# Block-sparse attention with a channel mix: dense units for the two blocks that see every key, two batches in one unit

## Chip, cores and metric

The kernel runs on one core of a Trainium2 chip. The metric is the device time of one execution in microseconds (us); the time before is the median of three runs.

## What is computed

```python
B, H, S, D = 4, 8, 768, 64          # block = 32, so 24 blocks
scores = (1 / sqrt(D)) * (q @ k.transpose(0, 1, 3, 2))
mask = |blk_i - blk_j| <= 1  or  blk_i in (0, 23)  or  blk_j in (0, 23)
for qb in range(24):                 # sampled_blocks: [24, 3], known only at run time
    mask[block qb, block kb] = True  for kb in sampled_blocks[qb]
attn = softmax(where(mask, scores, -1e9))
x = (attn @ v)  as  [B, S, H * D]    # 512 columns
xp = x shifted by one row, zero first
xk = mu_k * x + (1 - mu_k) * xp
xr = mu_r * x + (1 - mu_r) * xp
out = sigmoid(xr @ w_r) * (relu(xk @ w_k) ** 2 @ w_v)
```

Query blocks 0 and 23 see all 24 key blocks. Every other block sees at most eight: its own and its two neighbours, blocks 0 and 23, and three sampled ones. The weights w_r, w_k and w_v arrive as float64 (2, 4 and 4 MB), and the kernel turns them into pairs of fp32r tiles.

## The kernel before

**Units.** Attention is cut into 24 units. A dense unit (`m == ALL`, `load_wide` and `wide_pair`) takes four query blocks of one batch, 128 rows, against all 768 keys; the blocks are `WIDE_BLOCKS`, which are 21, 22, 23 and 0, so there are four dense units, one for each batch b. A gathered unit (`load_near` and `near_unit`) takes two neighbouring query blocks of a pair of batches, also 128 rows, against the eight key blocks that each may see; ten units for each of the two pairs cover blocks 1 to 20.

**A dense unit** goes over four pairs of heads, hp. For each: scores `sw` (PE, one matmul per head and half of the keys), a masked minimum in `soft` (DVE) and the exponential (ACT), twelve transposes `tw` (PE) that are copied to `ptw`, then products with the values, `o_-1_...` (PE). At the end `finish` divides by the row sums and transposes four times, `tx`. **A gathered unit** has 32 score matmuls `s` (64 rows by 32 columns of the array each), `soft`, `exp`, sixteen transposes `t`, 64 value matmuls `o` and four `tx`. Its keys are laid in the tile `KR`, of which there is one: the next unit's keys can only be asked for when `s` of this unit is done. Its values take four of the six tiles `VR`.

**Transfers.** SP issues nearly all of them, in one order. A gathered unit is q (262 KB), the near keys `kd` (524 KB), six sampled key blocks `kt` (131 KB each, at addresses that SP reads from the tile `packed`), two near value tiles `vn` (524 KB) and six sampled value blocks `vt`; when a tile is first used for a pair, blocks 0 and 23 come as well. A dense unit is 3.4 MB: q, four key tiles `k_ring<-kq` of 393 KB, and six value transfers of 262 KB. SP stays at most 2.2 MB ahead of what has landed (`QUEUED`).

**Channel mix.** Each of 12 tiles (128 rows of a pair of batches) has PE work in three parts: gates `r` (w_r), hidden rows `h` (w_k), output rows `v` (w_v). A tile can start when the units of all its blocks are done and the weights it reads are converted; tile 0 of a pair needs block 0 and the units m = 0 and 1.

**Order.** `Plan` sorts all operations by ranks from hand-tuned tables (`UNIT_AT`, `TILE_AT`, offsets `O_...` and `W_...`) and by its own costs and buffer queues; each engine then runs its list in that fixed order. The units come in the order of `UNITS`:

```python
UNITS = [
    (0, ALL), (1, ALL), (2, ALL), (0, 0), (0, 1), (3, ALL), (0, 2), (0, 3), ...
]
```

Dense units of the second pair are thus done early, and their rows for that pair's tiles are parked in HBM (`away`) and read back later.

Of the kernel before, what the change touches and what calls it, by code (L numbers as in the profile page):

```python
# [26 lines left out]
TT = 128  # L27
# [14 lines left out]
WIDE_SCALE = 2.0**-8  # L42

# [54 lines left out]
class Plan:  # L98
# [168 lines left out]
def block_sparse_attention_channel_mix(  # L267
    ctx: ExitStack, tc: tile.TileContext,
    kt, kd, kq, qw, qn, vt, vn, blocks, own_wide, own_near, mu_k, mu_r, w_k, w_v, w_r, out, wide,
# [34 lines left out]
    away = [Fixed(dr.tile([P, CC, P], F32, name=f"away{b}")) for b in range(PAIR, B)]


    def mask_setup():
# [35 lines left out]
        def twice():
# [3 lines left out]
            g = f.ap[:, 1:, :]  # L347
# [15 lines left out]
        plan.add(DVE, 1150, -30, far, reads=[(own,)], writes=[(f, 0), (same,), (wide_mask,)])  # L363
        plan.add(DVE, 2900, TWICE, twice, reads=[(con,)], writes=[(f, 1), (same,), (near_mask,)])
# [744 lines left out]
```

## Time and profile before

| | |
|---|---|
| three runs | 576.47, 576.67, 579.05 us (median 576.67) |
| profiled execution | span 575.5 us, from its first to its last instruction; its own time is not given apart, and the fastest and the median run lie 1.0 and 1.2 us above this span |
| PE (TensorE matmul) | 557.4 us busy, 97% of the span |
| DVE, ACT, POOL | 293.3, 298.2, 297.6 us busy, 51 to 52% |
| transfers | 102.91 MB, mean 179 GB/s |

PE is the matmul pipe, PEld its weight loads, which overlap with it. SPq rows are transfers that SP issues. A PE instruction counts as busy from its start to its modelled end, so neighbours overlap by 0.07 us or so; from the start of one group to the start of the next is what the group takes.

### The profile page before, as it was taken

Reading aid. Unit: us, or ns where it says so; the run is one execution under the profiler, and the core shown is the slowest. Engines: PE = TensorE matmul, PEld = TensorE weight load, DVE = VectorE, ACT = ScalarE, POOL = GpSimd, SP = SyncE. Lnnn points to the kernel's source line nnn. Section 1 sums busy time; section 2 is a strip of 40 time slices with the busy share of each in tenths; the row PEclk is TensorE's granted clock in tenths of the full one; section 3 lists DMA queues with packets and bytes.
Section 4 is the critical chain, followed back from the end, with each engine's and each line's share of the span. In section 5 each row is a group of like instructions: output and inputs, shape, how many; then the busy total and the mean of one; then the engine's idle time right before and its main releaser. Section 6 shows DMA issues by size and latency. Waiting matters only on the chain.

```text
span 575.5 us, 18316 instructions
## 1 busy us (share of the span) xinstructions
PE 557.4 (97%) x7203; PEld 461.1 (80%) x7203; DVE 293.3 (51%) x855; ACT 298.2 (52%) x719; POOL 297.6 (52%) x367
## 2 busy tenths in 40 slices
PE   8999877999999999999999999999999999999997
PEld 4777655788889888889889879888989888888886
DVE  4978786878872643445556454546314323230201
ACT  4688755758853736536736634544523344414420
POOL 0143546766655715607607605635428778867720
PEclk9999998999999999999999999999999999999999
DMA  8997789688898747766776577476302100010001
GB/s 297 403 305 270 233 279 344 210 269 298 266 288 251 208 144 211 229 206 200 236 220 194 174 238 228 143 234 182 97 20 84 39 0 1 17 45 12 2 18 56
DMA packets 52152, 102.91 MB, mean 179 GB/s; under 512 B 9345, under 2 KB 26626, under 8 KB 52066
## 3 DMA queue, kind: packets, MB, share of 16 engines
q1 hardware_dynamic: 51778, 101.51, 54.8%
q8 instruction: 57, 0.93, 0.6%
q14 instruction: 29, 0.24, 0.1%
q10 hardware_dynamic: 288, 0.22, 0.1%
HBM read 94.89 MB, written 6.82 MB: 177 GB/s over the span
## 4 chain that ended last, share of the span: by engine, by line
PE 80%; DVE 2%; POOL 1%; ACT 0%; issue 0%
PE v L895 24%; PE t L581 6%; PE o L643 6%; PE s L612 5%; PE r_0p L835 5%; PE r_1p L835 4%; PE h_1p L861 4%; PE h_2p L861 4%; PE h_0p L861 4%; PE h_3p L861 4%; PE tx L705 1%; PE o_-1_1567 L686 1%; PE h_1p L877 1%; PE h_5p L877 1%; PE h_4p L877 1%; PE r_3p L835 1%
## 5 line engine op out<-in xcount | busy, mean ns | idle before, releaser
L895 PE MATMUL v<-wv,k 128*128 128x512 f32 (+1 forms) x600 | 139.8, 389 | 0.3 <-ACT z L842 0.3
L895 PEld LDWEIGHTS v<-wv,k 128*128 128x128 f32 x600 | 108.2, 188 | 27.0 <-issue 1.6
L570 ACT ACTIVATE p<-p,nm 128x256 f32<-128x256 f32 x160 | 79.4, 498 | 15.1 <-DVE nm L560 15.0
L587 DVE COPY pt<-t 128x512 f32<-128x512 f32 x80 | 53.2, 684 | 59.7 <-PE t L581 48.3
L560 DVE CUSTOM_DVE_ANT_1 p<-s,near_mask 128x256 f32<-128x256 f32 x160 | 57.8, 419 | 14.0 <-PE s L612 10.7
L903 DVE SCALAR_TENSOR_TENSOR z<-v,z 128x512 f32<-128x512 f32 (+1 forms) x25 | 16.7, 670 | 71.8 <-PE v L895 52.6
L811 POOL TENSOR_TENSOR xr<-xr_1f,xr 128x256 fp32r<-128x256 f32 x24 | 18.2, 758 | 67.6 <-ACT xr L809 67.5
L581 PE MATMUL t<-ident,p 128*128 128x128 f32 x320 | 48.5, 285 | 4.0 <-DVE pt L587 2.4
L581 PEld LDWEIGHTS t<-ident,p 128*128 128x128 f32 x320 | 44.4, 206 | 6.8 <-ACT xt L720 1.7
L612 PE MATMUL s<-KR,q 64*32 64x256 f32 x1280 | 40.3, 379 | 2.1 <-DMA KR<-kt 1.9
L643 PEld LDWEIGHTS o<-VR,pt 128*32 128x32 f32 x2560 | 37.0, 110 | 5.3 <-issue 2.9
L643 PE MATMUL o<-VR,pt 128*32 128x64 f32 x2560 | 40.9, 220 | 0.2 <-DMA VR<-vt 0.2
L802 DVE SCALAR_TENSOR_TENSOR xr_1f<-xr_1d,mk,xt 128x128 f32<-128x128 f32 x48 | 19.5, 445 | 40.6 <-POOL xr L811 36.0
L802 DVE SCALAR_TENSOR_TENSOR xr_0f<-xr_0d,mk,xt 128x128 f32<-128x128 f32 x48 | 20.0, 452 | 33.0 <-POOL xr L811 28.3
L570 ACT ACTIVATE pw<-pw,nmw 128x768 f32<-128x768 f32 x32 | 30.0, 938 | 12.2 <-DVE nmw L560 12.1
L612 PEld LDWEIGHTS s<-KR,q 64*32 64x32 f32 x1280 | 24.6, 106 | 10.7 <-DMA KR<-kt 2.5
L835 PE MATMUL r_0p<-wr,xr 128*128 128x512 f32 x120 | 31.0, 403 | 0.0
L835 PE MATMUL r_1p<-wr,xr 128*128 128x512 f32 x120 | 30.5, 401 | 0.0
L570 ACT ACTIVATION_READ_ACCUMULATOR p<-p,nm 128x1 f32 x160 | 30.0, 188 | 0.0
L664 PE MATMUL sw<-k_ring,qw 64*128 64x384 f32 x128 | 27.5, 539 | 2.5 <-DVE x L708 1.1
L581 PE MATMUL tw<-ident,pw 128*128 128x128 f32 x192 | 27.7, 281 | 2.2 <-ACT ptw L585 1.6
L581 PEld LDWEIGHTS tw<-ident,pw 128*128 128x128 f32 x192 | 20.6, 141 | 10.6 <-ACT ptw L585 3.7
(188 smaller groups left out, 1079.5 us busy)
## 6 DMA issues: line engine op xcount, KB each, us to landing
VR<-vn SPq DMA_DIRECT2D x40, 512.0 KB, 4.6
VR<-vt SPq DMA_DIRECT2D x127, 128.0 KB, 4.0
KR<-kt SPq DMA_DIRECT2D x120, 128.0 KB, 3.3
KR<-kd SPq DMA_DIRECT2D x20, 512.0 KB, 4.2
VR<-vt SPq DMA_DIRECT2D x24, 256.0 KB, 7.0
out<-z SPq DMA_DIRECT2D x23, 256.0 KB, 2.3
k_ring<-kq SPq DMA_DIRECT2D x15, 384.0 KB, 6.1
q<-qn SPq DMA_DIRECT2D x20, 256.0 KB, 3.6
```

The lines of the kernel that those rows point to most:

```text
L560: nc.vector.tensor_tensor_reduce(out=p.ap[:, cs].rearrange("p (x n) -> p x n" if inner else "p (n x) -> p n x", **cut), in0=view().rearran ...
L570: plan.add(ACT, 378 + 0.83 * (cs.stop - cs.start), rank, lambda: nc.scalar.activation(p.ap[:, cs], p.ap[:, cs], AF.Exp, bias=nm.ap[:, col ...
L581: nc.tensor.transpose(tp.ap[:, i, :], cs(p.ap), ident.ap)
L587: plan.add(DVE, 690, rank + 0.1, lambda: nc.vector.tensor_copy(out=pt.ap, in_=tp.ap), reads=[(tp,)], writes=[(pt,)])
L612: nc.tensor.matmul(s.ap[ROWS[j], row, a * 256 : (a + 1) * 256].rearrange("p (x a g) -> p g a x", g=2, a=QB), q.ap[half, hp, ROWS[j]], eigh ...
L643: nc.tensor.matmul(o.ap[ROWS[j], h * D : (h + 1) * D], held[gi][i // 2].ap[:, 2 * (i % 2) + g, ROWS[j]], VR[values[j % PAIR][g]].ap[:, j / ...
L664: nc.tensor.matmul(s.ap[:, row, 0:W], q.ap[half, hp, :], K.ap[half, n0 * BLK : n0 * BLK + W], start=True, stop=True)
L802: nc.vector.scalar_tensor_tensor(out=part(f.ap[:, i, :]), in0=part(d.ap), scalar=mk.ap[:, which, c : c + 1], in1=x.ap[:, two, c, 0:TT], op ...
L811: plan.add(POOL, 80 + 2.4 * MIX * tw, rank + O_MIX, lambda f=f, cs=cs: nc.gpsimd.tensor_tensor(out=dst.ap[:, 1, cs], in0=f.ap, in1=dst.ap[ ...
L835: nc.tensor.matmul(pr.ap[:, 0:512], xr.ap[:, a, c, :], wr.ap[:, w, c, :], start=(c == 0 and m == 0), stop=(c == CC - 1 and m == 2))
L861: nc.tensor.matmul(ph.ap[:, ff * PAIR * TT : (ff + 1) * PAIR * TT], wk.ap[:, w, c, f * P : (f + 1) * P], xk.ap[:, a, c, :], start=(c == 0 ...
L895: nc.tensor.matmul(pv.ap[:, 0:width], hid[f][2](a), wv.ap[:, w, f, cs], start=(f == 0 and m == 0), stop=(f == FC - 1 and m == 2))
```

## The change

1. `WIDE_BLOCKS` is (23, 0). Blocks 21 and 22 become an eleventh gathered unit of each pair. A dense unit now takes blocks 23 and 0 of both batches of a pair: 128 rows again, but with the keys and the values of two batches, 6.6 MB. There are two dense units instead of four and 22 gathered ones instead of 20.
2. In a dense unit's scores each matmul covers 64 rows and 64 columns of the array (one batch), so there are four per half of the keys and not two; its value matmuls keep their number and shape and read each half of the columns from another batch's tile.
3. `UNITS` is in plain order: dense unit, then the eleven gathered ones, for each pair. The second dense unit's keys go into `KR` and its values into `VR`, which the gathered units use too. Nothing is parked in HBM any more.
4. `soft` of a gathered unit writes its probabilities so that a transpose reads 128 neighbouring columns (before: every second one).
5. `early` (the space of w_v before w_v is converted) holds keys and values of the second gathered unit; the first twelve raw weights use the `xt` tiles instead. All ranks are new numbers, and the planner's costs for transfers are.

```diff
-WIDE_BLOCKS = (NB - 3, NB - 2, NB - 1, 0)
+WIDE_BLOCKS = (NB - 1, 0)
-NP, NM = B // PAIR, (NB - QB) // PAIR
+NP, NM = B // PAIR, (NB - 2) // PAIR
...
-    FIRST, WORDS, AHEAD, ASKED, FETCHED = 143, 256, 298, 800, 2500
+    FIRST, WORDS, AHEAD, ASKED, FETCHED = 143, 256, 298, 800, 1600
-    RING, RATE, DONE, LANES = 650, 290, 800, 8
+    RING, RATE, DONE, LANES = 1600, 390, 1000, 8
...
-UNITS = [
-    (0, ALL), (1, ALL), (2, ALL), (0, 0), (0, 1), (3, ALL), (0, 2), (0, 3), (0, 4), (0, 5), (0, 6), (0, 7),
-    (0, 8), (0, 9), (1, 0), (1, 1), (1, 2), (1, 3), (1, 4), (1, 5), (1, 6), (1, 7), (1, 8), (1, 9),
-]
+UNITS = [(p, m) for p in range(NP) for m in [ALL, *range(NM)]]
...
+    v_ring = buf([P, V_RING, S], F32, "mixed", 1, "v_ring")
...
-            raw = Part(early, EARLY_W, ...) if i < 3 * CC else buf([P, 512, 2], I32, "p", P_BUFS, f"raw{i}")
+            raw = buf([P, 512, 2], I32, *(("xt", XT_BUFS) if i < 3 * CC else ("p", P_BUFS)), f"raw{i}")
...
+    def wide_key(lead, n):
+        if lead:
+            return Place(Part(k_ring, K_RING, lambda x, i: x[:, i]), [(0,), (1,)], lambda x: x)
+        k = n % K_LATER
+        slots[0][0] = None
+        return Place(KR[0], [(RINGS[k],)] * 2, lambda x: x.rearrange("p n b x -> p (n b x)")[:, k * S : (k + 1) * S])
+    def wide_value(lead, n):
+        if lead:
+            return Place(Part(v_ring, V_RING, lambda x, i: x[:, i]), (0, 1), lambda x: x)
+        w = n % VR_BUFS
+        slots[1][w] = None
+        return Place(VR[w], (0, 1), lambda x: x.rearrange("p b x -> p (b x)")[:, 0:S])
...
             if inner:
+                by = mask().unsqueeze(1).to_broadcast([P, BLK, SLOTS]).rearrange("p x (a g) -> p x a g", g=2)
+                cut = lambda x: x.rearrange("p (x a g) -> p x a g", g=2, a=QB)
+                dealt = lambda x: x.rearrange("p (g x a) -> p x a g", g=2, a=QB)
...
-                parts = [(p, [(i, i * 256)], lambda x, i=i, g=g: x[:, i * 256 : (i + 1) * 256].rearrange("p (y g) -> p g y", g=2)[:, g]) for i in (2 * a, 2 * a + 1) for g in range(2)]
+                parts = [(p, [(i, i * 256)], lambda x, i=i, g=g: x[:, i * 256 + g * P : i * 256 + (g + 1) * P]) for i in (2 * a, 2 * a + 1) for g in range(2)]
...
-                for row, half in enumerate(HALF):
-                    nc.tensor.matmul(s.ap[:, row, 0:W], q.ap[half, hp, :], K.ap[half, n0 * BLK : n0 * BLK + W],
-                                     start=True, stop=True)
+                for one, K in zip(HALF, both):
+                    for row, half in enumerate(HALF):
+                        nc.tensor.matmul(s.ap[one, row, 0:W], q.ap[half, hp, one], K.ap[half, n0 * BLK : n0 * BLK + W],
+                                         start=True, stop=True, skip_group_check=True)
...
-EARLY_W, EARLY_K, K_RING = 4, 0, 5
+EARLY_K, K_RING, V_RING, K_LATER = 2, 5, 5, 4
...
 UNIT_AT = [
-    -75.8943, -50.8142, -29.7091, -3.8416, 4.4692, 49.253, 88.5915, 99.3214, 124.6571,
+    -5.4147, 11.3186, 19.3007, 40.5254, 71.6051, 80.3593, 93.0373, 105.2062, 131.9685,
```

**Where instructions stand.** On PE, at the end of the first dense unit, before: the unit's last values (`o_-1_180`) and its `tx` stand among the scores and transposes of the second dense unit (its query tile is `qw_155`).

```order
L686 MATMUL o_-1_180<-VR_71,ptw_3_2_402 64x64 x4
L686 MATMUL o_-1_180<-VR_72,ptw_3_2_402 64x64 x4
L581 MATMUL tw_0_1_466<-ident,pw_0_0_339 128x128 x2
L581 MATMUL tw_0_1_466<-ident,pw_0_1_349 128x128 x2
L581 MATMUL tw_0_2_475<-ident,pw_0_1_349 128x128 x4
L664 MATMUL sw_2_0_487<-k_ring,qw_155 128x384 x2
L705 MATMUL tx_-1_494<-ident,x_-1_490 128x128 x4
L581 MATMUL tw_1_0_517<-ident,pw_1_0_472 128x128 x4
L664 MATMUL sw_2_1_522<-k_ring,qw_155 128x384 x2
L664 MATMUL sw_3_0_532<-k_ring,qw_155 128x384 x2
```

The same place after the change: behind the first dense unit's last values and `tx` come the scores of the first two gathered units (`s_0`, `s_1`).

```order
L710 MATMUL o_-1_174<-v_ring,ptw_3_2_476 64x64 x8
L729 MATMUL tx_-1_507<-ident,x_-1_502 128x128 x4
L635 MATMUL s_0_0_513<-KR_67,q_0_324 32x2x4x32 x16
L635 MATMUL s_0_1_545<-KR_67,q_0_324 32x2x4x32 x16
L604 MATMUL t_0_0_0_596<-ident,p_0_0_565 128x128 x4
L604 MATMUL t_0_0_1_613<-ident,p_0_0_565 128x128 x4
L604 MATMUL t_0_1_0_638<-ident,p_0_1_592 128x128 x4
L635 MATMUL s_1_0_647<-early,q_1_494 32x2x4x32 x16
L635 MATMUL s_1_1_677<-early,q_1_494 32x2x4x32 x16
L604 MATMUL t_0_1_1_698<-ident,p_0_1_592 128x128 x4
L666 MATMUL o_0_756<-VR_68,pt_0_0_0_610 32x64
```

Between the first dense unit and the first gathered one there were two more dense units; now there is nothing. On SP, before, some ten transfers into the list, the second dense unit's keys and values follow the first's:

```order
L476 DMA qw_155<-qw 128x512
L490 DMA k_ring<-kq 128x768 x2
L314 DMA number<-blocks 1x144
L316 DMA con<-own_near 128x190
L391 DMA early<-w_r 128x1024
L490 DMA k_ring<-kq 128x768
L498 DMA VR_73<-vt 128x512 x2
L498 DMA VR_74<-vt 128x512 x2
L498 DMA VR_75<-vt 128x512 x2
L476 DMA qw_317<-qw 128x512
```

After: behind the one dense unit's last tiles come raw weights and the first gathered unit's keys, whose sampled blocks need an address each (`TENSOR_LOAD`).

```order
L379 DMA raw_295<-w_k 128x1024
L526 DMA q_0_324<-qn 128x512
L516 DMA v_ring<-vw 128x768
L317 DMA con<-own_near 128x209
L379 DMA raw_367<-w_r 128x1024
L534 DMA KR_67<-kd 128x1024
L542 DMA KR_67<-kt 128x2x256
L456 TENSOR_LOAD packed
L456 ISA x2
L545 REGISTER_ALU
L545 ISA
L545 DMA KR_67<-kt 128x256
```

The first gathered unit's keys stood behind the transfers of two dense units and part of a third, and now stand behind those of one. Further down SP's list after the change come, in this order: a raw weight; the second gathered unit's q and keys with another raw weight among them; two raw tiles of w_v and the two small `mk` tiles; the first unit's values with a raw weight among them; q of unit 2; the second unit's values; the third unit's keys with a raw weight among them. On PE `s` of unit 2 stands behind the values and `tx` of unit 1, and the first `r` of tile 0 amid the values of unit 2.

## Rows read from the trace of the kernel before

**Rows 1.** Windows, whole span: stretch, us; busy us (x instructions) by engine; PEclk; DMA share; GB/s.

```profile
0.00:73.20 73.20, 68.35 (x972) 47.49 (x972) 55.52 (x182) 53.18 (x112) 23.60 (x28) 1.00 0.87 303
73.20:140.00 66.80, 58.81 (x1033) 47.20 (x1032) 52.76 (x141) 43.08 (x108) 41.50 (x46) 0.97 0.85 278
140.00:430.00 290.00, 287.94 (x4303) 248.75 (x4288) 148.22 (x468) 155.06 (x413) 140.37 (x180) 1.00 0.65 201
430.00:575.50 145.50, 142.29 (x915) 117.63 (x913) 36.77 (x68) 46.87 (x88) 92.11 (x114) 1.00 0.08 27
```

**Rows 2.** Timeline, PE, dense units: start us, us, line, operation, xcount.

```profile
0.78 4.85 PE L374 MATMUL idle<-const-bfloat16-1.0 128*128 128x512 bf16 x11 [0.78 <-PEq L1055]
5.56 1.67 PE L664 MATMUL sw<-k_ring,qw 64*128 64x384 f32 x8
...
40.79 1.56 PE L664 MATMUL sw<-k_ring,qw 64*128 64x384 f32 x8
...
45.44 1.56 PE L664 MATMUL sw<-k_ring,qw 64*128 64x384 f32 x8
```

**Rows 3.** Timeline, PE, a gathered unit's parts amid the channel mix.

```profile
262.04 1.96 PE L612 MATMUL s<-KR,q 64*32 64x256 f32 x64
...
270.79 1.99 PE L643 MATMUL o<-VR,pt 128*32 128x64 f32 x128
272.72 3.08 PE L861 MATMUL h_3p<-mixed,wk 128*128 128x256 f32 x24
275.64 0.60 PE L705 MATMUL tx<-ident,x 128*128 128x128 f32 x4
276.07 0.64 PE L581 MATMUL t<-ident,p 128*128 128x128 f32 x4
```

**Rows 4.** Groups by line and form, PE: busy us, mean ns, idle before.

```profile
L581 PE MATMUL t<-ident,p 128*128 128x128 f32 x320 | 48.5, 285 | 4.0 <-DVE pt L587 2.4 <-ACT xt L720 1.5
...
L612 PE MATMUL s<-KR,q 64*32 64x256 f32 x1280 | 40.3, 379 | 2.1 <-DMA KR<-kt 1.9 <-issue 0.2
...
L581 PE MATMUL tw<-ident,pw 128*128 128x128 f32 x192 | 27.7, 281 | 2.2 <-ACT ptw L585 1.6 <-DVE ptw L587 0.4 <-ACT pw L570 0.2
L664 PE MATMUL sw<-k_ring,qw 64*128 64x384 f32 x128 | 27.5, 539 | 2.5 <-DVE x L708 1.1 <-DVE nmw L560 1.1 <-DVE nm L560 0.3
```

**Rows 5.** Groups by line and form, weight loads.

```profile
L581 PEld LDWEIGHTS t<-ident,p 128*128 128x128 f32 x320 | 44.4, 206 | 6.8 <-ACT xt L720 1.7 <-DVE pt L587 1.6 <-ACT p L570 1.1
...
L581 PEld LDWEIGHTS tw<-ident,pw 128*128 128x128 f32 x192 | 20.6, 141 | 10.6 <-ACT ptw L585 3.7 <-issue 3.3 <-ACT pw L570 1.0
```

**Rows 6.** Windows, start of the span (the last figure is GB/s).

```profile
0.00:8.00 8.00, 6.67 (x21) 2.50 (x23) 2.36 (x10) 1.28 (x1) 0.76 (x7) 1.00 0.71 210
8.00:16.00 8.00, 7.56 (x76) 4.81 (x76) 5.46 (x20) 5.49 (x12) 0.00 (x0) 1.00 1.05 409
```

**Rows 7.** Timeline, SP's transfers: keys of two gathered units, values of one.

```profile
22.42 0.33 SPq L515 DMA_DIRECT2D KR<-kd  x1
...
31.41 0.42 SPq L391 DMA_DIRECT2D early<-w_r  x1
...
61.88 0.33 SPq L515 DMA_DIRECT2D KR<-kd  x1
...
67.36 0.42 SPq L476 DMA_DIRECT2D qw<-qw  x1
...
69.88 0.51 SPq L544 DMA_DIRECT2D VR<-vt  x1
...
73.44 0.50 SPq L544 DMA_DIRECT2D VR<-vt  x1
```

**Rows 8.** Tile KR, 20 to 45 us: issue to landing.

```profile
DMA to landing us min/median/max: 2.7/4.2/7.7
```

**Rows 9.** Windows with the lowered clock (PEclk is the eighth column, before DMA share).

```profile
96.00:98.00 2.00, 2.00 (x7) 0.65 (x6) 0.57 (x2) 0.48 (x2) 1.58 (x2) 0.50 1.07 397
```

**Rows 10.** Timeline, PE, the scores of a dense unit in that window.

```profile
94.94 2.93 PE L664 MATMUL sw<-k_ring,qw 64*128 64x384 f32 x8 [1.15 <-DVE x L708]
```

More of the change, by code (lines that the diff above doesn't have):

```diff
@@ L42, with wire @@
 WIDE_SCALE = 2.0**-8
+def wire(size, row):
+    return size * (1 + 195 / row)
 class Buf:
@@ L361, in twice @@
             v.scalar_tensor_tensor(out=m, in0=s_, scalar=-FAR, in1=m, op0=ALU.mult, op1=ALU.add)
-        plan.add(DVE, 1150, -30, far, reads=[(own,)], writes=[(f, 0), (same,), (wide_mask,)])
-        plan.add(DVE, 2900, TWICE, twice, reads=[(con,)], writes=[(f, 1), (same,), (near_mask,)])
+        plan.add(DVE, 2900, TWICE, twice, reads=[(con,)], writes=[(f,), (same,), (near_mask,)])
         for w, m in enumerate((mu_k, mu_r)):
@@ L462, in place_value @@
         turns[kind] += 1
-        return 2 * ((turns[kind] - 1) % (VR_BUFS // 2)) + kind
+        first = len(VR) // 2
+        return 2 * (turns[kind] - 1 if turns[kind] <= first else (turns[kind] - 1 - first) % (VR_BUFS // 2)) + kind
     def sampled_block(n, j):
@@ L503, in load_near, with __init__, ap @@
-    def load_near(pr, m, at):
+    class Place:
+        def __init__(self, owner, keys, view):
+            self.owner, self.keys, self.view = owner, keys, view
+        @property
+        def ap(self):
+            return self.view(self.owner.ap)
+    RINGS = [("ring", k) for k in range(K_LATER)]
+    NEAR_KEYS = ["near", ("far", 0), ("far", 1)]
+    def wide_key(lead, n):
[4 more added lines that the diff above has]
+        return Place(KR[0], [(RINGS[k],)] * 2, lambda x: x.rearrange("p n b x -> p (n b x)")[:, k * S : (k + 1) * S])
@@ L651, in near_unit, with wide_pair @@
                      writes=[(o, gi) for gi in mine], table="values", words=128 * len(mine))
-    def wide_pair(b, hp, q, K, values, o, L, t0):
+    def wide_pair(b, hp, q, both, values, o, L, t0):
         ps_ = [buf([P, S], F32, "p", P_BUFS, f"pw{b}_{hp}_{r}") for r in range(2)]
@@ L684, in pv @@
                 for n, i in enumerate(mine):
-                    for half in HALF:
+                    for one, V in zip(HALF, values):
                         nc.tensor.matmul(
-                            o.ap[half, h * D : (h + 1) * D], pts[i // 4].ap[:, i % 4, half],
-                            VR[values[n // 2]].ap[:, n % 2, h * D : (h + 1) * D], start=(n == 0), stop=(n == 5),
+                            o.ap[one, h * D : (h + 1) * D], pts[i // 4].ap[:, i % 4, one],
+                            V.ap[:, n * P + h % 2 * D : n * P + (h % 2 + 1) * D], start=(n == 0), stop=(n == 5),
                             skip_group_check=True)
-            plan.add(PE, 700, t0 + W_PV + 0.05 * row, pv, reads=[(pts[i // 4],) for i in mine[::2]] + [(VR[w], 0, 1) for w in values],
+            plan.add(PE, 700, t0 + W_PV + 0.05 * row, pv, reads=[(pts[i // 4],) for i in mine[::2]] + [(V.owner, *V.keys) for V in values],
                      writes=[(o, (hp, row))], table="halves", words=48)
@@ L1011 @@
 LAST, XT_BUFS = 5, 6
-PACE = {"wide": 0.91, "raw": 0.94, "value": 0.92}
 WARM = 10
@@ L1057 @@
     q, k, v, sampled = inputs["q"], inputs["k"], inputs["v"], inputs["sampled_blocks"]
-    of = np.array([WIDE_BLOCKS] + [[PAIR * m + 1 + j for j in range(PAIR)] * PAIR for m in range(NM)])
+    of = np.array([[PAIR * m + 1 + j for j in range(PAIR)] * PAIR for m in range(NM)])
     row = np.repeat(of, BLK, axis=1).T
-    near = row[:, 1:, None]
+    near = row[:, :, None]
     seen = np.concatenate([0 * near, 0 * near + NB - 1, near - 1, near, near + 1], axis=2)
     twice = np.zeros((P, NM, SLOTS))
-    twice[:, :, 3] = np.where(row[:, 1:] == 1, -FAR, 0.0)
-    blk = np.arange(NB)[None, :]
-    r = row[:, :1]
-    always = (np.abs(r - blk) <= 1) | (r == 0) | (r == NB - 1) | (blk == 0) | (blk == NB - 1)
-    own = con(sampled[row]).view(np.int32).reshape(P, NM + 1, NRAND * 2)
+    twice[:, :, 3] = np.where(row == 1, -FAR, 0.0)
+    twice[:, :, 7] = np.where(row == NB - 2, -FAR, 0.0)
+    own = con(sampled[row]).view(np.int32).reshape(P, NM, NRAND * 2)
     def beside(of, *more):
```

235 lines of the change are left out of this document (113 added, 122 removed).

## The prediction

> **What bounds the kernel now.** I read the windows first. PE is busy 68.35 of the first 73.2 us, 58.81 of the next 66.8, 287.94 of the 290 from 140 to 430, and 142.29 of the last 145.5 [rows 1]. So PE's own work sets the time, and its idle time stands in three places: 12.8 us before 140 us, 2.1 in the long middle, 3.2 at the very end, after its last matmul. Then the timeline of the start: eleven dummy matmuls of 4.85 us, and from 5.56 us on dense units without a break [rows 2]. While these run, the transfers fill up behind them: from 8 to 16 us they move 409 GB/s [rows 6]. The span is then
>
> lead 5.6 + PE's work 552.5 + waits 14.1 + tail 3.2 = 575.5 us (rounded),
>
> where the work is 557.4 us busy (the sum of rows 1) less the dummies' 4.85, and the waits are the idle time less the lead's 0.78 and the tail. I predict by the same four terms.
>
> **PE's work.** A dense unit passes from the scores of one pair of heads to the next pair's in 45.44 - 40.79 = 4.65 us [rows 2]; four pairs and `tx` (276.07 - 275.64 = 0.43 [rows 3]) make 19.0. A gathered unit takes 1.9 for `s` (1.96 less some 0.07 of overlap), 1.93 for `o` (to the start of the next) [rows 3], 16 transposes at 48.5 / 320 = 0.152 us [rows 4], 2.4, and `tx` 0.43: 6.6 us. Two dense units less: -38.0. Two gathered ones more: +13.2. The channel mix is unchanged.
>
> The transposes read in a row: the strided weight loads of `t` take 206 ns, the contiguous ones of `tw` 141 [rows 5], but these overlap with matmuls, and what a transpose takes of PE is 0.152 us for `t` and 27.7 / 192 = 0.144 for `tw` [rows 4]. I price the edit at that difference: 352 x 0.0073 = -2.6. Its bounds are 0 and, if every load lay bare, 352 x 0.065 = -22.9; `tw` has the short load already and passes hardly faster, so the value lies by the first. The new writes of `soft` (three dimensions, 176 instructions) appear nowhere in this trace. DVE is busy 148 of 290 us in the middle [rows 1], so they are hidden there; at the start each unit waits for two or three of them in a row, and if they took twice as long that would be a few us in all. A gain has no place to come from. I take 0 and keep +3 for the range.
>
> The dense scores in quarters of the array: per half of the keys, four matmuls of 64 x 64 instead of two of 64 x 128. If both column halves run at once, nothing changes; if they take turns, the 1.56 us that a pair of heads needs [rows 2] doubles, 8 times, about +12. The gathered scores cut the array in four column strips and pass 1280 records of 379 ns in 40.3 us [rows 4], twelve at a time, so strips do run at once. I take 0.
>
> Work after: 552.5 - 38.0 + 13.2 - 2.6 = 525.1 us, 27.4 less. Had PE been fed as before, that would be the gain.
>
> **The waits at the start.** What fed PE up to 73 us was three dense units: 3.4 MB for 19.0 us of PE. The new one needs 6.6 MB for 19.0, a gathered one 3.4 MB for 6.6, and the mix cannot start without unit 1 and the converted weights. So I follow the new list of transfers in time. By 8 us 8 x 0.210 = 1.68 MB have landed, then 0.409 MB per us [rows 6].
>
> The dense unit, eight raw weights and q are 11.1 MB: landed at 31 us. The last value tile goes into a ring slot that the second pair of heads frees, and is among the last of these, so the dense unit ends at about 31 and not at 25. SP is 2.2 MB ahead, so it reaches the first gathered keys when 9.4 MB have landed, at 27. From here on SP's pace counts, because each sampled block is an issue of its own. First keys of a pair: 31.41 - 22.42 = 9.0 us (about a raw weight's issue of slack is in it) [rows 7], to 36; they land 2.7 later (the least of [rows 8]: at SP's pace no queue stands in front of them); `s` of unit 0 at 39. A q and a raw weight at 0.6 each, then 9.0 again for unit 1: 46; `s` at 49. Three raw weights and two small tiles, 3.0, and unit 0's values, 2 x (73.44 - 69.88) = 7.1 [rows 7]: 56; `o` at 59. q and unit 1's values, 7.7: 64; `o` at 67. Keys of unit 2, 67.36 - 61.88 = 5.5 [rows 7], and a raw weight: 70; **`s` of unit 2 at about 73 us**. That is 24.4 MB, or 0.35 MB per us from 8 us on, under the rate of rows 6: the transfers could bear it.
>
> At that point PE has done one dense unit and two gathered ones, 19.0 + 13.2 = 32.2 us, and has waited 73 - 5.6 - 32.2 = **35.2 us**. Before, it had waited 4.1 by then [rows 1].
>
> From 73 us on the first gate `r`, the first `h` and units 2 and 3 give PE work. By SP's pace unit 2's values (2 x 2.85, a fifth less than with the extra block) let `o` run at 79, unit 3's `s` comes at 86, unit 4's at 98. Between 73 and 98 stand on PE: all of unit 2 (6.6), `s` and `t` of unit 3 (4.3), an `r` and two `h` (2.9 each: 275.64 - 272.72 [rows 3]), 19.6 us, so 5.4 more of waiting. Behind 98 us each `s` has 10 us or more of `h`, `o`, `r` or `v` in front of it and SP needs 12 for a unit, some of it early; I find no long wait, nor at the second dense unit: its keys have some 10 us of PE work between the freeing of `KR` and their use, its values more. I put 2 us for all of it, as in the 290 us of rows 1.
>
> The clock: at 96 to 98 us, after waits, the granted clock was 0.50 [rows 9], which is the 1.2 GHz level, and the scores that take 1.56 us took 2.93 [rows 10]. The new start is idle half of the time, so I expect the low level there. What is slowed while PE waits for data costs nothing; what is slowed after 73 us does. Unit 2 at half rate is 6.6 us more, half of it inside the 5.4 of waiting: I take +3, between 0 and +11.
>
> Waits after: 35.2 + 5.4 + 2 + 3 = 45.6, for 14.1 before. Sum: 5.6 + 525.1 + 45.6 + 3.2 = 579.5 us of span, 4.0 over before. The median run lies 1.2 over the span: **581 us**, 0.7% slower. The 27.4 us of work taken from PE are lost again, and a little more, because the work taken away was what covered the transfers at the start.
>
> **A rule weighed against the rows.** The rows show 409 GB/s over 8 us [rows 6]. The Trainium skill (DMA: Bandwidth & Descriptors, Specifications) gives about 358 GB/s as the limit that HBM sets for a core. By the page's figure, as an estimate, 24.4 MB land at 71 us at the earliest, and the fast start of rival B gives 2 us at most; by the row it gives 9. The row decides here.
>
> On the clock, rows 9 and 10 agree with the Trainium skill (TensorE: Matmul & The Clock Gate, HAM oscillation): a kernel that waits for transfers between short bursts of matmuls pays the slow clock at burst after burst. That is the mechanism of rival C.
>
> **Rivals.**
> A, the forecast, 577 to 586: SP's pace sets the start. Chance 0.45.
> B, faster: transfers run at 0.409 MB per us up to unit 2's keys. 24.4 MB have then landed at 8 + 22.7 / 0.409 = 63.5 us, 9.5 less waiting: 571.5. For it: SP's list lets it run 2.2 MB ahead. Against: the key issues of rows 7 move 1.8 MB in 9 us. It decides if unit 2's `s` starts before 66 us. Chance 0.17.
> C, the clock stays low up to 98 us: 19.6 us of work take 39.2 in a stretch of 25, 14 more instead of 3: 592. Against: before, with 8 us of waits between 73 and 140 us, the mean clock of that stretch is still 0.97 [rows 1]. Chance 0.1.
> D, the dense scores' halves take turns: +12, 593. Rows 4 speak against it. 0.06.
> E, faster: the strided loads did cost PE their time; up to 20 us less, 561 to 574. For it: 206 against 141 ns [rows 5]. Against: [rows 4]. 0.07.
> F, a wait in the middle: the second dense unit's values go into `VR` slots that unit 10 must free, and SP, which is blocked at them, also brings the next unit's keys; 3 to 8 us more, 584 to 589. 0.15.
>
> **Numbers.** 581 us. 570 to 591 leaves out the half of E, and D and C, 0.19 in all; A alone is 577 to 586. A difference of 0.5% is about what a measurement of this kernel can tell from none, so "same" is 573.8 to 579.6: the low part of A (0.17), the ends of B and E (0.07). Faster is the rest of B and E, 0.17, and I give 0.19; slower the rest, 0.57.
>
> **What would show it.** In the trace after: `s` of unit 2 at 73 us (66 or less: B), PE idle about 35 us before it, spread over gaps between 31 and 73; the granted clock at 0.5 in parts of 35 to 85 us; from 100 us on PE as full as before; PE's busy time near 525 plus the dummies and what the low clock adds; `t` at 0.144 us each; the dense scores' stretch 1.56 us. The prediction is wrong if PE's idle time before 100 us is under 30 us, or if a long wait appears after it.

## The result and the profile after

The kernel after takes 583.54 us (median of five runs, 579.79 to 585.80), the kernel before, timed beside it, 576.67 (576.31 to 579.05): a ratio of 1.0101, 95% interval 1.0073 to 1.0130. It is 1% slower. The profiled execution has a span of 584.0 us and a time of 585.8; it is the slowest of the five, 2.3 us over the median. All times and ratios in this document leave out runs in a slower state of the chip; the only one among them was a run of E12 (591.52 us).

The windows of the kernel after, the same stretches as [rows 1]:

```profile
0.00:73.20 73.20, 47.03 (x611) 30.72 (x611) 48.82 (x128) 38.06 (x85) 32.53 (x37) 0.77 0.92 320
73.20:140.00 66.80, 55.23 (x1053) 43.08 (x1052) 52.71 (x132) 40.12 (x109) 44.84 (x49) 0.97 0.86 286
140.00:430.00 290.00, 288.20 (x4447) 242.57 (x4448) 162.03 (x460) 152.53 (x394) 131.20 (x169) 1.00 0.65 211
430.00:584.00 154.00, 150.33 (x1031) 124.56 (x1029) 44.92 (x103) 56.32 (x120) 93.22 (x114) 1.00 0.10 33
```

PE is busy 47.0 us of the first 73.2 (before 68.35), 55.2 of the next 66.8 (before 58.81), and from 140 us on it is as full as before. Its idle time grew from 18.1 to 43.2 us, and all but 0.2 us of the growth stands ahead of 140 us. The granted clock of the first stretch fell from 1.00 to 0.77. In windows of 8 us:

```profile
8.00:16.00 8.00, 5.69 (x44) 2.43 (x38) 3.78 (x15) 3.10 (x7) 0.00 (x0) 0.79 1.03 416
48.00:56.00 8.00, 4.47 (x56) 2.76 (x64) 7.52 (x17) 4.66 (x14) 4.07 (x6) 0.58 0.99 344
56.00:64.00 8.00, 1.60 (x34) 0.69 (x14) 7.55 (x23) 5.45 (x19) 4.16 (x4) 0.71 0.90 306
64.00:72.00 8.00, 7.04 (x141) 6.36 (x142) 3.82 (x8) 3.38 (x6) 5.27 (x5) 0.50 0.84 283
```

The last three columns are the granted clock, the busy share of the 16 DMA engines, and GB/s. The DMA engines are 0.84 to 1.03 busy in all four, yet move 416 GB/s in the first and 283 in the last. The timeline of PE in the same time (start, length; in brackets the idle time before it and what ended it):

```profile
38.50 1.11 PE L604 MATMUL tw<-ident,pw 128*128 128x128 f32 x4 [4.02 <-DVE ptw L610]
...
43.17 0.66 PE L729 MATMUL tx_-1_507<-ident,x_-1_502 128*128 128x128 f32 x4 [0.80 <-DVE x_-1_502 L732]
43.76 2.22 PE L635 MATMUL s<-KR,q 64*32 64x256 f32 x64
...
53.64 3.11 PE L635 MATMUL s<-early,q 64*32 64x256 f32 x64
...
64.17 3.63 PE L666 MATMUL o<-VR,pt 128*32 128x64 f32 x126 [5.11 <-DMA VR<-vt]
...
77.06 0.62 PE L635 MATMUL s<-KR,q 64*32 64x256 f32 x4
79.38 1.95 PE L635 MATMUL s<-KR,q 64*32 64x256 f32 x60 [1.70 <-DMA KR<-kt]
```

The dense unit ends at 43.8 us (predicted 31), `s` of unit 0 starts at 43.8 (39), of unit 1 at 53.6 (49), of unit 2 at 77.1 (73; 60 of its 64 matmuls wait for the last keys until 79.4). From one `s` to the next the steps are as walked (9.9 us for 10, 23.4 for 24); the dense unit's end is what was 13 us off, and unit 0's keys 5. SP's own queue says why (us in total, times, longest; 5 to 77 us):

```profile
SPq L516 <- PE o_-1_174 L710: 5.0, 2, 4.0
SPq L510 <- PE sw L688: 3.4, 1, 3.4
SPq L379 <- DVE wf L401: 2.4, 1, 2.4
```

Its transfers at that place, and what DVE does with `con`:

```profile
24.91 0.42 SPq L526 DMA_DIRECT2D q<-qn  x1
29.47 0.33 SPq L516 DMA_DIRECT2D v_ring<-vw  x1
...
32.06 0.43 SPq L534 DMA_DIRECT2D KR<-kd  x1
```

```profile
33.40 0.21 DVE L335 COPY near_mask<-con 128x88 f32<-128x88 f32 x1 [1.70 <-DMA con<-own_near]
...
37.76 1.28 DVE L610 COPY ptw<-tw 128x512 f32<-128x512 f32 x2
```

From 25 to 29.5 us SP stands before a value tile of the dense unit (L516), whose ring slot PE has yet to free. Behind it in the list wait the small table `con` and unit 0's keys, which start at 32.1 instead of 27. DVE reaches `con` late, computes `near_mask` from it, and only then copies the `ptw` for which the `tw` at 38.50 waits 4.0 us.

### The profile page after: what moved, and what is told of

Its sections match the earlier page's. It is cut to its first block, busy times and chain, and to the rows that moved or that the text cites. A ratio compares the mean times of both kernels' runs of the same rounds, so it can differ in the third digit from the quotient of the medians.

```text
span 584.0 us, 18180 instructions
## 1 busy us (share of the span) xinstructions
PE 540.8 (93%) x7139; PEld 440.9 (76%) x7139; DVE 308.5 (53%) x818; ACT 287.0 (49%) x705; POOL 301.8 (52%) x368
## 4 chain that ended last, share of the span: by engine, by line
PE 77%; DMA 8%; SPq 6%; DVE 4%; issue 3%; ACT 2%; ACTq 0%; DVEq 0%
PE v L906 23%; PE o L666 6%; PE s L635 5%; PE t L604 5%; PE r_1p L846 4%; PE r_0p L846 4%; PE h_2p L872 4%; PE h_3p L872 4%; PE h_1p L872 4%; PE h_0p L872 3%; SPq L565 2%; DMA raw<-w_v 2%; PE tw L604 2%; PE sw L688 2%; DVE p L584 2%
## 5 line engine op out<-in xcount | busy, mean ns | idle before, releaser
L593 ACT ACTIVATE p<-p,nm 128x256 f32<-128x256 f32 x176 | 87.3, 498 | 25.9 <-DVE nm L584 25.8
L584 DVE CUSTOM_DVE_ANT_1 p<-s,near_mask 128x256 f32<-128x256 f32 x176 | 89.1, 627 | 8.8 <-PE s L635 8.4
L610 DVE COPY pt<-t 128x512 f32<-128x512 f32 x88 | 58.4, 686 | 58.8 <-PE t L604 58.7
L604 PE MATMUL t<-ident,p 128*128 128x128 f32 x352 | 53.4, 285 | 9.5 <-ACT p L593 5.7
L666 PE MATMUL o<-VR,pt 128*32 128x64 f32 x2752 | 46.9, 224 | 7.2 <-DMA VR<-vt 7.0
L666 PEld LDWEIGHTS o<-VR,pt 128*32 128x32 f32 x2752 | 42.4, 113 | 14.2 <-issue 11.4
L635 PE MATMUL s<-KR,q 64*32 64x256 f32 x1344 | 44.5, 386 | 3.2 <-DMA KR<-kt 2.3
L813 DVE SCALAR_TENSOR_TENSOR xr_1f<-xr_1d,mk,xt 128x128 f32<-128x128 f32 x48 | 19.7, 445 | 35.1 <-POOL xr L822 28.1
L822 POOL TENSOR_TENSOR xr<-xr_0f,xr 128x256 fp32r<-128x256 f32 x24 | 17.7, 738 | 28.5 <-ACT xr L820 28.5
L744 ACT COPY xt<-tx 128x512 f32<-128x512 f32 (+2 forms) x32 | 13.5, 457 | 35.6 <-PE tx L729 35.6
L809 POOL TENSOR_TENSOR xr_1d<-xt 128x128 f32<-128x128 f32 x48 | 19.5, 417 | 22.1 <-DVE xr_1f L813 14.5
L732 DVE TENSOR_TENSOR x<-o,R 128x512 f32<-128x512 f32 x22 | 15.2, 689 | 25.0 <-PE o L666 25.0
```

The costliest lines, as they stand in the source:

```text
L584: nc.vector.tensor_tensor_reduce(out=dealt(p.ap[:, cs]), in0=cut(view()), in1=by, scale=-SCALE, scalar=3e38 if first is None else nm.ap[:, ...
L593: plan.add(ACT, 378 + 0.83 * (cs.stop - cs.start), rank, lambda: nc.scalar.activation(p.ap[:, cs], p.ap[:, cs], AF.Exp, bias=nm.ap[:, col ...
L604: nc.tensor.transpose(tp.ap[:, i, :], cs(p.ap), ident.ap)
L610: plan.add(DVE, 690, rank + 0.1, lambda: nc.vector.tensor_copy(out=pt.ap, in_=tp.ap), reads=[(tp,)], writes=[(pt,)])
L635: nc.tensor.matmul(s.ap[ROWS[j], row, a * 256 : (a + 1) * 256].rearrange("p (x a g) -> p g a x", g=2, a=QB), q.ap[half, hp, ROWS[j]], eigh ...
L666: nc.tensor.matmul(o.ap[ROWS[j], h * D : (h + 1) * D], held[gi][i // 2].ap[:, 2 * (i % 2) + g, ROWS[j]], VR[values[j % PAIR][g]].ap[:, j / ...
```

## Experiments

Theories as they stood: **A**, SP's pace sets the start (the forecast); **B2**, the transfers' own rate does, at 0.31 MB per us in this mix; **V**, the vector engines' work does (weight conversions, `soft`); **C2**, the low clock costs little, since it lies in the shade of waits. Ratios are to the kernel before on the same chip.

**E1 and E2: part 4 alone.** E1 takes it out of the kernel after, E2 puts it into the kernel before (the new writes of `soft`, and this):

```diff
-    x[:, i*256 : (i+1)*256].rearrange("p (y g) -> p g y", g=2)[:, g]
+    x[:, i*256 + g*P : i*256 + (g+1)*P]
```

> The kernel after with part 4 alone taken back: soft writes as before, the transposes read every second column; order and transfers are those of the kernel after. Theory S (the loss is made at the start by late transfers, an issue queue that stands still and a low clock; part 4 is a small gain on PE): t takes 0.149 us again in the middle instead of 0.140, 352 x 0.009 = 3 us more, 586.5 us. Rival W (the new writes of soft, 0.63 us instead of 0.42 on DVE, stand on the path at the start): five units in a row with two or three of them each give 2 to 3 us back, so the two cancel or it is faster, 581 to 583.5 us; PE's idle time before 100 us would be 2 to 3 us less.

> The kernel before with part 4 alone. Theory S: PE is the bound there, DVE has room, so the gain of the transposes is all there is: 320 x 0.009 = 2.9 us less, 573.8 us, and soft at 0.63 us costs nothing. Rival W: soft's longer writes take it back, 576 to 578 us. If every strided load lay bare (rival E of the prediction), 320 x 0.065 = 21 us less, 556 us.

E1: 583.87 us, ratio 1.0106 (1.0083 to 1.0128), as the kernel after. E2: 578.32 against 577.94 us, ratio 1.0001 (0.9978 to 1.0024). The transposes from 140 to 430 us, in the kernel before and in E2, and `soft` in E2 over the whole span:

```profile
L581 PE MATMUL t<-ident,p 128*128 128x128 f32 x256 | 38.2, 283 | 0.0
...
L585 PE MATMUL t<-ident,p 128*128 128x128 f32 x256 | 35.5, 273 | 0.0
...
L565 DVE CUSTOM_DVE_ANT_1 p<-s,near_mask 128x256 f32<-128x256 f32 x160 | 81.3, 631 | 13.2 <-PE s L616 9.8 <-PE t L585 3.1
```

256 transposes take 35.5 us of PE for 38.2 before, so the gain on PE is there (0.010 us each). `soft` takes 631 ns for 419, 23.5 us more on DVE. The time shows neither. Rival E is out (556 us). Part 4 is worth 0, with 1.4 us either way; whether a small gain and a small loss cancel or both are hidden, these two runs don't tell. In E2's profile all transposes together take 3.6 us less of PE (44.9 for 48.5), but PE is busy as long as before (557.0 us for 557.4) and idle 2.2 us longer (20.3 for 18.1), so there the gain was lost again elsewhere on PE; that `soft`'s longer writes took it is likely and not shown.

**E3: nothing queued behind the ring slot.**

```diff
-    plan.add(SP, ISSUE, -30, lambda: nc.sync.dma_start(con.ap, own_near), ...)
+    plan.add(ACT, ISSUE, -61, lambda: nc.scalar.dma_start(con.ap, own_near), ...)
-    due = -58.5 + hp + 0.1 * i if lead else ...
+    due = (11.747 if hp == HP - 1 and i else -58.5 + hp + 0.1 * i) if lead else ...
```

> The kernel after; the small table con is issued by ACT at the start and the last value tile of the first dense unit stands behind the first sampled keys of unit 0 in SP's list, so that nothing is queued behind a ring slot that PE must free. Theory S: SP reaches unit 0's keys at 25 to 27 us instead of 32, near_mask is ready before tw of the last pair of heads, the dense unit ends 4 to 5 us sooner and s of unit 2 starts at about 72 us instead of 77: 578.5 us. Rival B2 (from 25 us on the transfers' own rate, not SP's list, sets the pace): the same bytes land at the same time, s of unit 2 stays at 76 to 77 us, 583 us.

588.53 us, ratio 1.0195 (1.0163 to 1.0227): slower than the kernel after. Unit 0's keys start at 25.4 us, as meant, but `s` of unit 2 at 77.9. A line of PE, and SP's waits:

```profile
39.18 2.82 PE L710 MATMUL o_-1_174<-v_ring,ptw 128*64 128x64 f32 x46 [4.34 <-DMA v_ring<-vw]
```

```profile
SPq L379 <- DVE wf L401: 5.9, 2, 3.4
SPq L379 <- POOL wf L412: 4.6, 2, 3.1
...
SPq L516 <- PE o_-1_174 L710: 1.4, 1, 1.4
```

The wait for the ring slot is gone (1.4 us for 5.0); in its place the raw weights wait 10.5 us (2.4 before) for their `xt` tiles, which conversions on DVE and POOL must free (part 5 gave twelve raw weights six tiles). One wait at the head of SP's list gave way to the next. The edit also has a price of its own: the dense unit's last values now wait 4.3 us for the tile that was put back, so its `tx` starts at 44.5 us, no sooner than in the kernel after (43.2).

**E4: the clock held up.** Dummy matmuls in PE's planned gaps:

```diff
-SPIN_END, SPIN, ... = -117.5187, ...
+SPIN_END, SPIN, ... = 76.0, ...
```

> The kernel after with dummy matmuls of 128 x 512 in the planned gaps on PE up to 76 us (some 60 of them), which compute nothing that is used. Theory S: the granted clock stays at 0.9 or more up to 76 us, the 8 to 11 us that PE's work takes longer there at the low clock come back, as far as they do not end in a wait for transfers: 575 to 579 us. Rival C2 (what is slowed lies in the shade of the waits for data): PE's own work is shorter, its waits are longer by as much, 582 to 584 us.

586.10 us, ratio 1.0144 (1.0121 to 1.0166). The window to 73.2 us:

```profile
0.00:73.20 73.20, 56.93 (x793) 34.77 (x796) 53.39 (x132) 39.62 (x87) 35.00 (x38) 0.91 0.92 327
```

```profile
77.30 2.74 PE L635 MATMUL s<-KR,q 64*32 64x256 f32 x60 [2.27 <-DMA KR<-kt]
```

The granted clock is 0.91 for 0.77. Of the 56.9 us 18.4 are dummies (4.5 in the kernel after), so PE's own work up to there takes some 4 us less. `s` of unit 2 starts at 74.4 us, and most of it at 77.3 after a wait for its keys. C2 holds: the work that ran faster brought no time, and the run is 2.5 us slower than the kernel after. A part of that may be the dummies' own doing, since they stand in PE's order: unit 0's values start at 61.7 us behind 5.9 us of them.

**E5: a third of the issues.** Three blocks as one transfer, the first sampled one and the two behind it (keys shown; values likewise, and these lie in neighbouring rows of their tile, where each block had every fourth row):

```diff
+    if pr == 0 and m <= 6:
+        nc.sync.dma_start(K.ap[:, (NRAND + 1) * j : (NRAND + 1) * j + NRAND]...,
+                          kt[bass.ds(sampled_block(n + j, 0) + pr * NB, NRAND)]...)
+        return
```

> The kernel after; in units 0 to 6 of the first pair the three sampled blocks of a group are taken as one transfer of three neighbouring blocks (the first sampled one and the two behind it, so other keys and values than the reference's): the same bytes in rows of the same length, with 4 issues for 12 and without two thirds of SP's address arithmetic. Forecast A (SP's pace sets the start): SP is done with unit 2's keys about 15 us sooner, s of unit 2 at 62 to 67 us instead of 77, 569 to 575 us. Theory B2 (the DMA engines are busy over 0.9 of this time and pass their bytes at 0.31 to 0.35 MB per us whoever issues them): they can gain a tenth at most, s of unit 2 at 70 to 75 us, 578 to 583 us.

588.57 us, ratio 1.0184 (1.0151 to 1.0217). Its PE timeline, SP's last transfer of unit 0's values in E5 and (three as one row) in the kernel after, and the window from 48 to 73.2 us, E5 first and the kernel after behind it:

```profile
65.94 3.64 PE L676 MATMUL o<-VR,pt 128*32 128x64 f32 x126 [5.37 <-DMA VR<-vt]
...
78.78 2.13 PE L645 MATMUL s<-KR,q 64*32 64x256 f32 x64
```

```profile
56.95 0.34 SPq L570 DMA_DIRECT2D VR<-vt  x1
...
57.75 2.22 SPq L565 DMA_DIRECT2D VR<-vt  x3
```

```profile
48.00:73.20 25.20, 13.26 (x219) 9.30 (x218) 18.83 (x49) 14.29 (x41) 13.17 (x13) 0.61 1.01 304
```

```profile
48.00:73.20 25.20, 14.31 (x224) 10.59 (x224) 20.10 (x49) 13.82 (x38) 13.72 (x14) 0.59 0.91 311
```

SP is done with unit 0's values at 57.3 us, 2.7 sooner, and `o` of unit 0 starts 1.8 us later (65.9 for 64.2). The DMA engines go to 1.01 busy, and they move no more: 304 GB/s for 311. So the transfers can hardly pass faster than SP asks for them in the kernel after, with E5's rows at least. Unit 2's keys tell less: the first is issued 2.5 us sooner (66.8 for 69.3), but then SP stands 4.2 us before a raw tile of w_v that transposes must free, and the second half follows at 74.5, as before the edit (74.1). That SP's own pace is no bound does not follow: in the kernel after SP waits for something in only 3.3 of the 44 us from 32 to 76, and E9 below bears on it.

**E6: half the bytes from unit 2 on.** `part` is 64 of 128 rows for units 2 to 6:

```diff
-    K.ap[:, WINDOW : WINDOW + 4]..., kd[pr, :, n - 1 : n + 3]...
+    K.ap[0:part, WINDOW : WINDOW + 4]..., kd[pr, 0:part, n - 1 : n + 3]...
```

> The kernel after; for units 2 to 6 of the first pair the key and value transfers (not q) move half of the rows, so that the rest of these tiles holds older data: the same issues, half the bytes. Theory B2: unit 2's keys land 2 us sooner and each later unit some 4 us sooner than the one before it, the 10 us or so that PE waits between 73 and 140 us mostly go: 573 to 578 us. Forecast A: SP issues as before, the same time, 582 to 585 us.

590.27 us, ratio 1.0233 (1.0196 to 1.0270). From 73.2 to 100 us the DMA share falls to 0.73 (before the edit 0.90), from 100 to 140 to 0.62 (0.84), and PE is no fuller (18.1 us for 20.1 up to 100). So behind unit 2's keys B2 does not hold, as far as a run can say whose granted clock is lower there (0.89 and 0.90, the kernel after 1.00 and 0.96). On the start, which the edit hardly touches, it says nothing.

**E7 and E8: PE work taken out of the kernel before, at two places.** E7 leaves out value products in the first three dense units, E8 in sixteen gathered units:

```diff
-    for n, i in enumerate(mine):
+    for n, i in enumerate(mine[:1] if b < 3 else mine):
```

```diff
+    less = b == 1 or m >= 4
-    for g in range(2):
+    for g in range(2 - less):
```

> The kernel before; the first three dense units leave out five sixths of their value products (only the first of six key groups is summed): 3 x 5.5 = 16.6 us of PE's work less before 73 us, no transfer less. Theory B2 (there PE's work is the cover of the transfers): PE waits instead, the time falls by 0 to 5 us, 572 to 578 us. If PE's work sets the time there too, it falls by 16 us, 561 us.

> The kernel before; sixteen gathered units (all of the second pair, m = 4 to 9 of the first) leave out one half of their value products, 64 of 128 at 16 ns: 16 x 1.02 = 16.4 us of PE's work less, nearly all of it between 120 and 430 us, no transfer less. Both theories: PE sets the time there, the time falls by 14 to 16.4 us, 561 to 564 us. It would fall by less if the transfers (0.65 busy there) or the chain of a unit became the bound.

E7: 573.89 us for 577.40, ratio 0.9940 (0.9920 to 0.9960), 3.5 us less. E8: 561.67 us, ratio 0.9723 (0.9693 to 0.9754), 16 us less. One of E7's three units, and E8's gathered units, by form, each behind its row of the kernel before:

```profile
L686 PE MATMUL o_-1_180<-VR,ptw 128*64 128x64 f32 x192 | 6.7, 224 | 0.0
...
L686 PE MATMUL o_-1_180<-VR,ptw 128*64 128x64 f32 x32 | 2.0, 237 | 0.0
```

```profile
L643 PE MATMUL o<-VR,pt 128*32 128x64 f32 x2560 | 40.9, 220 | 0.2 <-DMA VR<-vt 0.2
...
L644 PE MATMUL o<-VR,pt 128*32 128x64 f32 x1536 | 28.1, 228 | 1.2 <-DMA VR<-vt 1.2
```

The three units' products took 6.7, 6.7 and 6.5 us before and take 2.0, 2.0 and 1.8 in E7; the gathered ones took 40.9 and take 28.1 in E8. So E7 took 14.1 us off PE, E8 12.8 (16.4 by the count of matmuls at 16 ns). The same kind of work is worth a quarter of its length at the start and all of it in the middle. This is the clearest pair of the study: the dense units of before were cover. What E7 loses again is not waiting alone: PE is idle 4.0 us longer (22.1 for 18.1), and its busy time as a whole falls by only 9.2 us (548.2 for 557.4), with the granted clock at 0.79 to 1.00 between 56 and 88 us, where it was 1.00.

**E9, E10 and E12: relief of the start.** Half of the rows for units 0 and 1 and the dense unit's last tiles (E9); for units 0 to 6, with E5's issues (E10); with E11's edit too (E12). **E11** leaves the shift and the sign out of the conversions:

```diff
-    nc.sync.dma_start(r.ap, kw[pr, hp, :, i])
+    nc.sync.dma_start(r.ap[0:half], kw[pr, hp, 0:half, i])
...
+    part = P // 2 if pr == 0 and m <= 1 else P
```

```diff
-    plan.add(DVE, 425, rank, shift, ...)
+    less = lambda f: lambda: None
+    plan.add(DVE, 425, rank, less(shift), ...)
```

> The kernel after; the key and value transfers of units 0 and 1 and the last three key and value tiles of the first dense unit move half of their rows (the other rows hold zeros or older data): the same issues, 4.8 MB less before unit 1's values. GpSimd, idle there, clears the other rows at the start. Theory B2 (the transfers' own rate sets the start up to 77 us): 4.8 MB at 0.31 MB per us are 15 us; SP's pace then takes over, so s of unit 2 at 64 to 70 us instead of 77 and 574 to 579 us. Forecast A (SP's pace alone): the issues are the same, s of unit 2 stays at 75 to 77 us and the time at 582 to 586 us. Theory V (the weights' conversions and soft on DVE, ACT and GpSimd set the start): s of unit 2 moves by less than 3 us.

> The kernel after; half of the rows as in the run before, for units 0 to 6 of the first pair, and their sampled blocks three to an issue: half the bytes and a third of the issues of these units together. If transfers and SP are all that holds the start (B2 and A together), s of unit 2 comes at 55 to 62 us, PE's waits before 140 us fall from 40 to some 20 us, 562 to 570 us. Theory V: the conversions and the chain of each unit on DVE and ACT hold it next, s of unit 2 may come sooner but PE's waits before 140 us stay over 30 us, 576 to 584 us.

> The kernel after; the conversion of the weights leaves out the shift and the sign on DVE (20 and 8 instructions, 0.55 and 0.93 us, 18 us of DVE's 100 busy between 20 and 140 us), so the weights are wrong; transfers and PE's work are the same. Theory V: DVE, 80% busy from 24 to 100 us, is what unit 2's and 3's soft, pt and the mix's first split wait for: 575 to 580 us. Theory B2: up to 77 us nothing changes, after it 0 to 3 us, 581 to 584 us.

> The two runs before in one: half the bytes and a third of the issues for units 0 to 6, and the conversions without shift and sign. Whatever of transfers, SP's issues and DVE's conversions holds the start is eased here at once. If these are all, PE's waits before 140 us fall from 40 to 15 us or less and the time is 558 to 566 us, near the 27 us that PE's work became shorter. If it stays over 575 us, something else holds the start: the fixed order of the instructions, or the clock.

Measured: E9 587.44 us, ratio 1.0153 (1.0127 to 1.0178); E10 585.10, 1.0137 (1.0102 to 1.0172); E11 583.93, 1.0110 (1.0088 to 1.0133); E12 585.28, 1.0127 (1.0083 to 1.0171).

E11 takes 18 us off DVE's busy time. `s` of unit 2 starts so:

```profile
74.62 0.62 PE L636 MATMUL s<-KR,q 64*32 64x256 f32 x4
77.48 3.55 PE L636 MATMUL s<-KR,q 64*32 64x256 f32 x60 [2.23 <-DMA KR<-kt]
```

That is 2.4 and 1.9 us sooner than in the kernel after; E6, which has the same start up to unit 2's keys, has 75.4 and 77.9, so the spread between runs is nearly as large. The ratio is the kernel after's. As far as DVE's conversions go, V is not what holds the time.

E9, E10 and E12 gained nothing either. E10's window says why it doesn't count against B2:

```profile
48.00:73.20 25.20, 12.66 (x239) 7.99 (x219) 19.95 (x54) 15.05 (x44) 14.70 (x15) 0.64 0.98 200
```

Half of the rows move at 200 GB/s with the DMA engines 0.98 busy. A packet takes 16 x 25.2 x 0.970 / 2172 = 180 ns, in the kernel after 16 x 25.2 x 0.904 / 3366 = 108, at the same mean size (2.3 KB); E10's row first:

```profile
## 3 DMA queue, kind: packets, MB, share of 16 engines
q1 hardware_dynamic: 2172, 4.99, 97.0%
...
q1 hardware_dynamic: 3366, 7.79, 90.4%
```

Rows 0 to 63 alone take nearly as long as all 128, so E10 took bytes away and hardly any transfer time; E12 is like it (1.05 busy, 212 GB/s). The Trainium skill (SBUF — State Buffer, Door 1: The DMA port swizzle) states that rows 0 to 63 reach eight of the 16 ports and pass at some 218 GB/s at most; the 200 of E10, a third of it raw weights and q in all 128 rows, agrees.

E9 did ease the DMA engines and left SP its issues. Its windows, the one of the kernel after from 24 to 48 us, and the first keys of units 0 and 2 on SP, E9 and then the kernel after:

```profile
24.00:48.00 24.00, 14.35 (x188) 11.91 (x196) 16.53 (x36) 13.85 (x24) 15.63 (x14) 0.70 0.75 222
48.00:73.20 25.20, 13.96 (x264) 8.90 (x248) 19.47 (x54) 15.70 (x45) 15.06 (x15) 0.64 0.85 217
...
24.00:48.00 24.00, 14.98 (x240) 11.88 (x239) 19.02 (x47) 14.52 (x30) 18.07 (x17) 0.79 0.91 308
```

```profile
35.33 0.47 SPq L541 DMA_DIRECT2D KR<-kd  x1
...
74.88 0.57 SPq L541 DMA_DIRECT2D KR<-kd  x1
```

```profile
32.06 0.43 SPq L534 DMA_DIRECT2D KR<-kd  x1
...
69.29 0.57 SPq L534 DMA_DIRECT2D KR<-kd  x1
```

SP takes 39.6 us from the one to the other, in the kernel after 37.2, though the DMA engines are 0.75 and 0.85 busy for 0.91 and 0.91. With the transfers eased SP's list is no faster: this speaks for A. E9, E10 and E12 also start late: `s` of unit 0 at 47.3, 45.7 and 45.7 us, 1.9 to 3.5 behind the kernel after. In E9 the stretch from 16 to 24 us, with the dense unit's half tiles in it, already moves 230 GB/s (367), and ACT stands 2.6 us before a raw weight that has not landed, with the exponential and the copy behind it for which `tw` at 26.7 us waits; that this is the whole delay is not shown.

## Why the prediction came out right, and where it was wrong

**The size.** Forecast 581 us, measured 583.54, inside 570 to 591 and inside A's own 577 to 586; "slower" had 0.57. The range takes the result in with room on both sides.

**PE's work, 525.1 us: right.** Busy time is 540.8, less 4.5 of dummies 536.3. Where the granted clock c was below 1, I take busy x (1 - c) as lost, window by window of 8 us up to 120: some 12 us, an estimate, which leaves 524 to 525. Two dense units less and two gathered ones more are worth what the rows said, and E8 shows that PE work taken away in the middle is paid in full.

**The transposes, -2.6 us: right on PE, 0 in the time.** The 0.010 us of each is there; E1 and E2 show no change of time.

**`soft`'s new writes, 0 with +3 kept: open.** The price on DVE was not foreseen: 627 ns in the kernel after for 420 in E1, 176 times. E1 and E2 move it together with the transposes and show that both together are worth nothing that can be measured; that the writes alone cost nothing they don't show.

**The dense scores, 0: right.** The second dense unit, at full clock:

```profile
L688 PE MATMUL sw<-KR,qw 64*64 64x384 f32 x64 | 6.1, 495 | 0.0
```

6.1 / 4 = 1.52 us for a pair of heads, as in [rows 2]. Both column halves run at once; rival D is out.

**The waits, 45.6 us: near in sum; the room above SP's pace was wrong.** With the estimate above the profiled run waited 584.0 - 5.6 - 524.5 - 3.7 = 50 us, clock included; 39.3 of it (77.1 - 5.6 - 32.2) before unit 2's `s`, where 35.2 were predicted, and 11 behind it, where 10.4 were. The forecast named the 35.2 as idle time, and PE is idle for 26 of the 39.3; in the other 13 its work took longer than the 32.2 us forecast, most of that at the low clock, while it had to wait anyway. Before 100 us PE is idle for 32.9 us; under 30 was named as a sign of being wrong.

The walk along SP's list held from unit 0's keys on: SP hardly waits there (3.3 of 44 us), and E9 shows its list at the same pace with the DMA engines eased. What was wrong is the sentence "the transfers could bear it", as far as it gives them room above that pace. It took the 0.409 MB per us of [rows 6], measured on the dense units' and weights' long rows, for the sampled keys and values too. The mix with those passes at 283 to 345 GB/s with the DMA engines 0.84 to 0.99 busy; from 0 to 77 us the kernel moves 24.5 MB, 0.32 MB per us. E5 shows that fewer issues don't help. SP's pace and the transfers' rate lie side by side here, and no run eased both at once. That a walk which gave the transfers room came within 4 us was therefore luck in part: had they been a little slower, they and not SP would have set the time. Rival B named the right second resource at a rate that this mix doesn't reach, so its 571.5 us could not come. The prediction weighed 358 GB/s of the Trainium skill (DMA: Bandwidth & Descriptors, Specifications) against 409 of the row. 8 us at 416 again lie above the page's figure, and the start lies below it with SP's pace as one bound, so neither number gave the time.

**The dense unit's end, 31 us: wrong by 13.** The ring slot was seen, but taken as a wait of that tile alone; SP's list stands still behind it, and `con` with it. Two more parts of it were not in the walk: at 33.1 us `tw` waits 2.3 us for an exponential that stands behind four weight conversions on ACT, and the granted clock is 0.72 to 0.79 from 24 to 40 us. Eight of the 13 us fall into a wait that was there anyway, since unit 0's keys were due at 39; its `s` is 4.8 us late and unit 2's 4.1.

**The clock, +3 of 0 to 11: right in place.** 0.50 to 0.71 between 48 and 72 us, 1.00 from 80 to 100. Of the 12 us that PE's work is longer, by the same estimate, under 2 lie behind 72 us; the rest lies ahead of unit 2's keys, and E4 won no time by taking some 4 us of it back. Rival C (592 us) did not come.

**Rival F: no.** 288.20 busy of 290 from 140 to 430 us; the second dense unit has no wait of note.

**The main reason holds.** The work taken away was cover. E7 shows the other side of it in the kernel before: 14 us of the same work left out at the start bring 3.5.

**Open.** Why the mix with the sampled keys and values passes at 283 to 345 GB/s and not at 416 is not settled; rows of 1 KB (the keys) may be part of it, the value rows are 4 KB. An edit that eases the transfers over all 128 rows was not tried, and none that eases them and SP's issues together, so how much of the start is SP's, how much the transfers' and how much the chain from unit to unit is argued from E5, E9, E11, E4 and the waits in the profile. Why E3, E5 and E6 are about 5 us slower than the kernel after, with `s` of unit 2 within 2 us of the same time, is only argued: their granted clock over the run is lower (0.956 to 0.968, the kernel after 0.962 to 0.979), and from 73.2 to 100 us they run at 0.81, 0.85 and 0.89, the kernel after at 1.00.

## What to carry to other kernels

Price PE work that is taken away by what waits at its place: at the start, where transfers fill in behind it, 14 us were worth 3.5, in the middle all. Compare units there by PE time per byte that they need. Take a transfer rate from the same kind of transfer (rows, tiles, number in flight), not from the best window of the trace. Before an experiment is read, see in its own profile that it eased the resource that it was meant to ease: E10 halved the bytes and left the DMA engines 0.98 busy. And where two bounds lie side by side, easing one (E5 the issues, E9 the transfers) shows no gain and acquits neither.

## What was not expected of the hardware

- Transfers to 64 of 128 rows: 180 ns for a packet of 2.3 KB, for 108 with all rows; 200 GB/s at a DMA share of 0.98.
- `soft` with its output dealt out to two halves 128 columns apart: 627 to 631 ns for 128 x 256, for 419 to 420 written in a row. The weight loads that read the result in a row take 141 ns for 206, and a transpose 0.139 us of PE for 0.149.
- Weight loads of 206 ns lie almost wholly beside the matmuls: 0.065 us less of each load brought PE 0.010.
